# First token list from six half batches instead of eight, the other confident columns in two parts

## The chip, the cores and the metric

The kernel runs on one core of one Trainium2 chip. The metric is the device time of one execution in microseconds (us). Before the change the median of three runs was 1246.0 us, the lowest 1242.64 and the highest 1251.04. One further execution was taken by the hardware profiler, and every duration below is from that one.

## The reference, cut to what matters

A causal seven-tap convolution over the sequence (eight heads of 24 channels, softmax weights) makes 28672 tokens of 192 channels. A router with eight experts gives each token to one expert, greedily by logit, with at most 3584 tokens per expert. Each token goes through the two-layer network of its expert.

```python
out = np.einsum('hk,bskhg->bshg', w, x_unf)            # causal convolution, 7 taps, 8 heads
...
cap = N // E                                           # 28672 // 8 = 3584
logits = x @ w_gate
order = np.argsort(-logits.flatten())
for idx in order:
    tok, e = (int(idx) // E, int(idx) % E)
    if assigned[tok] >= 0 or counts[e] >= cap:
        continue
    assigned[tok] = e
    counts[e] += 1
...
for e in range(E):
    mask = assigned == e
    h = np.maximum(x[mask] @ w1[e], 0.0)               # 192 -> 1024
    out[mask] = h @ w2[e]                              # 1024 -> 192
```

## The kernel before, in words

**Convolution.** The sequence is cut into 16 half batches of 1792 tokens. For each, eight matmuls (one per head, `cv<-X,TH` in the trace, two records each) make the convolution, ScalarE evicts it to `a`, and a DMA stores it to the DRAM tensor `attn`. VectorE transposes `a` to `aT`, TensorE makes logits from that (`pl<-aT`), transposes them (`pt`), and ScalarE writes them into the table `LT` [128 partitions, 8 experts, 256 columns]; each half batch fills 16 columns. `M1` holds the largest logit of each token.

**Routing.** A token whose largest logit is above a sampled threshold `Ts` is confident: it goes to its best expert whatever comes later. The lists of such tokens are made from the columns of `LT`, in parts. For a part, `settle` marks the confident tokens in `F`, `count` counts them per expert, `place` numbers them, `slots` splits the number into a place within 128 and a block, `sort` or `sort4` brings the tokens into that order with one-hot matmuls (VectorE builds the one-hots `oa`, TensorE multiplies), `gather` puts the pieces of all parts together in the table `asm`, and `tokens` turns them into row numbers: `ia` (row of the output) and `ja` (row of `attn`). `sort` is followed by `turn`, which transposes its result on TensorE. `sort4` instead writes its result to the DRAM table `otab` and reads it back transposed (`X<-otab`); `gather` must wait for that read. Its time is guessed by a constant, `TURN = 10.0`, from the last eviction.

Before the change there are two parts of 128 columns. The first part (eight half batches) gives the first list, of which 512 tokens per expert are used (`ia0`, `ja0`). The second part gives the complete confident list (`ia`, `ja`, 2048 per expert). Then `rest` settles all other tokens by seven rounds of threshold search on VectorE (`rounds`, `final`) and makes their list in two halves (`ib`, `jb`, 1536 per expert), each by `sort4`.

**The expert network.** The tokens go through the network in 56 tiles of 512 tokens: tiles 0 to 7 take the first list (one for each expert), tiles 8 to 31 the confident list (three for each), tiles 32 to 55 the rest. Tile i is done in eight steps (f): five matmuls of layer 1 of tile i (`ph`), then eight matmuls of layer 2 of tile i-1 (`y`). ScalarE makes `hh` from `ph`, VectorE `hl`; three buffers hold `ph`. GpSimd gathers the rows of a tile from `attn` two tiles ahead (`xg`), and scatters the results to the output. Weights of a new expert are loaded as `raw` pieces, split into two terms by ScalarE and VectorE or GpSimd, used, and kept in DRAM (`kw`, `kv`) for the later passes.

**What sets the order.** Every engine runs its instructions in the order in which the program writes them. The routing is a chain of generators (`Steps`): at fixed places, between the matmuls of the convolution and of the tiles, `hook` lets the first generator run on for a few steps, as long as a rough running estimate of the engines' times (`Pace`) says that VectorE is not more than a slack ahead of TensorE. So the estimate decides at build time where routing instructions stand among the others. Three places force the chain: before tile 6 gathers for tile 8, `bg.drain(1)` runs whatever is left of the confident list and one step of what follows; before tile 30 gathers for tile 32, `bg.drain()` runs all that is left of `rest`, and takes no account of `TURN`; before tile 1 the last logits are finished. In the convolution, the backlog of transposes and logits is held from half batch 13 on until the first list is made (`LAG`, `got`); then the rows of tiles 0 and 1 are gathered (`first`), and ten heads later, at heads 2 and 5 of a half batch, the operands of tile 0 are transposed on TensorE (`bg<-ident,xg`) and evicted (`todo`).

All instructions that go through the pace estimate carry line L56 in the profile, so they are told apart by the names of their tiles: `bg` is the PSUM tile of every routing matmul.

## Time and profile before

| what | before |
|---|---|
| median of three runs | 1246.0 us |
| profiled execution, its own time | 1251.99 us |
| span from first to last instruction in it | 1250.2 us |
| TensorE busy | 1208.1 us, 97% of the span |
| VectorE busy | 979.4 us, 78% |
| ScalarE busy | 547.4 us, 44% |
| GpSimd busy | 531.7 us, 43% |
| mean granted TensorE clock | 0.994 |

TensorE is nearly always busy, so a microsecond in which it waits, or has one more microsecond of work, is a microsecond at the end. A matmul's end is modelled in the records; how much time a run of matmuls takes is read from the start of the next one. In a timeline row the columns are the start, the busy time, the engine, the tiles (out<-in), the shape, the count, and in brackets the idle time before it and what ended it.

### The profile page before, as it was taken

What the parts mean: (1) busy time and instruction counts of PE and PEld (TensorE: products, weight loads), DVE (VectorE), ACT (ScalarE), POOL (GpSimd) and SP (SyncE); (2) the same over time, 40 slices, a digit from 0 to 9 for tenths busy, and PEclk for the clock granted to TensorE, in tenths of its full rate; (3) what the DMA queues carried; (4) which work ended last, traced back from release to release, by engine and by line L of the source; (5) the groups of instructions that cost most, each with busy time, mean ns of one, the idle gap of its engine ahead of it and who ended that gap; (6) DMA issues with size and microseconds to landing.
All of it is one profiled execution on the core that took longest, in us unless ns stands there. A gap on an engine that the chain in (4) does not pass through costs nothing.

```text
span 1250.2 us, 21752 instructions
## 1 busy us (share of the span) xinstructions
PE 1208.1 (97%) x7702; PEld 1036.5 (83%) x7702; DVE 979.4 (78%) x2131; ACT 547.4 (44%) x1220; POOL 531.7 (43%) x528
## 2 busy tenths in 40 slices
PE   4999989999999999999999989999999999999997
PEld 2445568889988989889888879999999999999996
DVE  7388669889898898989888865777777777777772
ACT  4454555656444544444543333333443333443331
POOL 3000344535455545555454434445444544444522
PEclk9999999999999999999999999999999999999999
DMA  9999889999725463444344563114133222413100
GB/s 221 339 348 310 294 299 316 280 321 302 270 82 155 128 188 113 158 149 149 123 144 135 178 164 121 36 48 154 67 126 107 95 97 96 157 56 137 49 23 28
DMA packets 125188, 205.09 MB, mean 164 GB/s; under 512 B 21440, under 2 KB 85392, under 8 KB 121360
## 3 DMA queue, kind: packets, MB, share of 16 engines
q1 hardware_dynamic: 82464, 127.22, 31.9%
q0 software_dynamic: 21504, 44.07, 11.7%
q10 hardware_dynamic: 21104, 32.34, 7.8%
q8 instruction: 62, 1.02, 0.3%
q14 instruction: 54, 0.44, 0.1%
HBM read 118.64 MB, written 84.93 MB: 163 GB/s over the span
## 4 chain that ended last, share of the span: by engine, by line
PE 85%; DVE 6%; DMA 5%; issue 1%; SPq 1%; ACT 1%; POOL 1%; ACTq 0%; POOLq 0%; DVEq 0%
PE ph L56 40%; PE y L56 38%; PE bg L56 3%; PE cv L56 3%; DMA X<-in_x_dram 2%; DVE X L56 1%; DVE aT L56 1%; DMA wgr<-in_moe_w_gate_dram 1%; DMA raw<-in_moe_w_dram 1%; DMA X<-otab 1%; PE pl L56 1%; DMA xg<-attn,ja 1%; DVE hl L56 0%; PE px L56 0%; DMA otab<-X 0%
## 5 line engine op out<-in xcount | busy, mean ns | idle before, releaser
L56 PE MATMUL y<-w,hh 128*128 128x384 f32 x1792 | 536.8, 355 | 0.0
L56 ACT ACTIVATE hh<-ph 128x512 fp32r<-128x512 f32 x448 | 267.2, 597 | 486.3 <-PE ph L56 485.2
L56 PE MATMUL y<-w,hl 128*128 128x192 f32 x1792 | 449.7, 251 | 0.0
L56 DVE SCALAR_TENSOR_TENSOR hl<-ph,hh 128x512 fp32r<-128x512 f32 x448 | 308.5, 689 | 138.6 <-ACT hh L56 134.0
L56 PE MATMUL ph<-xa,w 128*128 128x512 f32 x1344 | 395.6, 402 | 0.0
L56 PEld LDWEIGHTS y<-w,hl 128*128 128x128 f32 x1792 | 341.7, 191 | 16.4
L56 PEld LDWEIGHTS y<-w,hh 128*128 128x128 f32 x1792 | 337.1, 188 | 20.4 <-issue 2.2
L56 PEld LDWEIGHTS ph<-xa,w 128*128 128x128 f32 x1344 | 218.9, 189 | 20.2 <-issue 1.0
L1348 POOL DMA_INDIRECT out_dram<-yo,ia x128 | 138.9, 1085 | 225.9 <-DVE yo L56 188.1
L1348 POOL DMA_INDIRECT out_dram<-yo,ib x96 | 95.9, 999 | 220.1 <-DVE yo L56 212.7
L56 PE MATMUL ph<-xd,w 128*128 128x512 f32 x448 | 178.9, 399 | 1.3 <-DVE xd L56 1.3
L56 PE MATMUL ph<-xd,dl 128*128 128x512 f32 x448 | 174.6, 390 | 0.2 <-DVE dl L56 0.2
L56 DVE STREAM_TRANSPOSE xs<-xg 32x128 f32<-32x128 f32 (+2 forms) x408 | 164.8, 404 | 6.6
L1273 POOL DMA_INDIRECT xg<-attn,ja x128 | 139.3, 1088 | 47.6 <-issue 40.4
L56 PE MATMUL cv<-X,TH 118*128 118x384 f32 x256 | 101.5, 523 | 19.5 <-DVE TH L56 12.5
L1273 POOL DMA_INDIRECT xg<-attn,jb x96 | 103.4, 1078 | 29.3 <-issue 29.3
L56 ACT ACTIVATE yt<-y 128x192 f32<-128x192 f32 x224 | 73.1, 326 | 94.3 <-PE y L56 92.3
L56 DVE TENSOR_TENSOR yo<-y,yt 128x192 f32<-128x192 f32 x224 | 79.5, 355 | 41.3 <-ACT yt L56 39.2
L56 PEld LDWEIGHTS ph<-xd,w 128*128 128x128 f32 x448 | 84.3, 188 | 21.4 <-DVE xd L56 1.7
L56 PEld LDWEIGHTS ph<-xd,dl 128*128 128x128 f32 x448 | 84.5, 189 | 19.7 <-issue 0.5
L56 PEld LDWEIGHTS cv<-X,TH 118*128 118x128 f32 x256 | 45.3, 198 | 49.9 <-issue 14.1
L56 ACT ACTIVATE a<-cv 128x384 f32<-128x384 f32 x128 | 59.5, 492 | 50.8 <-PE cv L56 33.0
(238 smaller groups left out, 893.1 us busy)
## 6 DMA issues: line engine op xcount, KB each, us to landing
attn<-a ACTq DMA_DIRECT2D x16, 1344.0 KB
w<-kw SPq DMA_DIRECT2D x14, 1536.0 KB
w<-kv SPq DMA_DIRECT2D x14, 1536.0 KB
kw<-w SPq DMA_DIRECT2D x48, 256.0 KB
kv<-w SPq DMA_DIRECT2D x32, 384.0 KB
X<-in_x_dram SPq DMA_DIRECT2D x17, 672.0 KB
X<-in_x_dram ACTq DMA_DIRECT2D x15, 672.0 KB
scr<-xs SPq DMA_DIRECT2D x96, 96.0 KB
```

The lines of the kernel that those rows point to most:

```text
L56: return f(*a, **k)
L1273: self.nc.gpsimd.indirect_dma_start(out=t[:, b], out_offset=None, in_=self.attn[0:rows], in_offset=bass.IndirectOffsetOnAxis(ap=idx[b], ax ...
L1348: st = self.nc.gpsimd.indirect_dma_start(out=self.out, out_offset=bass.IndirectOffsetOnAxis(ap=idx, axis=0), in_=o, in_offset=None, bounds ...
```

## The change

The columns are cut at 96 and 224 (`PARTS`): the first part has the columns of six half batches, the second those of eight, the third those of the last two. `early` makes the first list from part one. `second` makes part two by `sort4`; while its read-back from DRAM is under way, `third` marks and counts part three (before the change, `open`, which takes the confident tokens out of `LT` and `F`, stood there); after the gather of part two, part three is placed, sorted by `sort` in 32 columns, turned and gathered, then `tokens` makes the list, and `open` comes last. `rest` keeps its two halves (`HALVES`). The other edits pass a column offset and a width instead of a half's number.

```diff
+PARTS = ((0, 96), (96, 128), (224, 32))
+HALVES = ((0, 128), (128, 128))
...
-        while z < 128:
+        n = part[1]
+        while z < n:
...
-                if z == 64:
-                    yield from self.columns(h, nt, base)
+                if z == n // 64 * 32:
+                    yield from self.columns(part, nt, bases)
...
             for u in range(4):
                 e = 4 * q + u
-                if base is not None:
-                    PE.matmul(o, b(self.tot[base]), self.ones, start=False, stop=False, skip_group_check=True)
-                PE.matmul(o, b(self.tot[h]), self.U, start=False, stop=(u == 3), skip_group_check=True)
+                for p in bases:
+                    m = p[1]
+                    PE.matmul(o, self.tot[p][:, e:e + 1].to_broadcast([m, 128]), self.ones[0:m, 0:n],
+                              start=False, stop=False, skip_group_check=True)
+                PE.matmul(o, self.tot[part][:, e:e + 1].to_broadcast([n, 128]), self.U[0:n, 0:n],
+                          start=False, stop=(u == 3), skip_group_check=True)
...
-    def lists(self, F, nt, h, base, idx, row, *part, between=None, swap=False):
-        yield from self.place(F, h, base)
-        yield from self.slots(F, h, between is None)
+    def listed(self, F, nt, part, bases, between=None):
+        yield from self.place(F, part, bases)
+        yield from self.slots(F, part, between is None)
         if between is None:
-            yield from self.sort(h, nt, base)
-            yield from self.turn()
+            yield from self.sort(part, nt, bases)
+            yield from self.turn(part[1])
         else:
-            yield from self.sort4(h, nt, base)
+            yield from self.sort4(part, nt, bases)
             yield from between
-        yield from self.gather(nt, base is None)
-        yield from self.tokens(nt, idx, row, *part, swap=swap)
+        yield from self.gather(part[1], nt, not bases)
...
-        def half(h):
-            if h == 0:
-                yield from r.thresh(0.905)
-            yield from r.settle(h)
-            yield from r.count(r.F, h)
-            if h:
-                yield from r.counts(NE)
-            yield from r.lists(r.F, TA, h, 0 if h else None, *((ia, ja) if h else (ia0, ja0, 8, 4)),
-                               between=r.open() if h else None, swap=h == 1)
+        def early():
+            yield from r.thresh(0.905)
+            yield from r.settle(PARTS[0])
+            yield from r.count(r.F, PARTS[0])
+            yield from r.listed(r.F, TA, PARTS[0], ())
+            yield from r.tokens(TA, ia0, ja0, 8, 4)
+
+        def second():
+            yield from r.settle(PARTS[1])
+            yield from r.count(r.F, PARTS[1])
+            yield from r.listed(r.F, TA, PARTS[1], PARTS[0:1], between=third())
+            yield from r.listed(r.F, TA, PARTS[2], PARTS[0:2])
+            yield from r.tokens(TA, ia, ja, swap=True)
+            yield from r.open()
+
+        def third():
+            yield from r.settle(PARTS[2])
+            yield from r.count(r.F, PARTS[2])
+            yield from r.counts(NE)
...
-        bg = Steps(nc, r, (half(0), tail(), half(1), rest()))
+        bg = Steps(nc, r, (early(), tail(), second(), rest()))
```

Since the pace estimate places the steps, the change moves instructions far from its own lines. Three places are shown, each before and after.

The first is TensorE at the end of the convolution. `cv` are the convolution's matmuls, `pl` and `pt` the logits' matmuls and transpose, `bg<-ident,xg` the transposes of tile 0's gathered rows, `ph` the first layer of tile 0. Before:

```order
L56 MATMUL pl<-aT,c_mu 32x128 x8
L56 MATMUL bg<-ident,xg 128x128 x4
L56 MATMUL cv<-X,TH 128x384
L56 MATMUL pl<-aT,c_mu 32x128 x8
L56 MATMUL cv<-X,TH 128x384
L56 MATMUL pt<-ident,L 128x128
L56 MATMUL bg<-ident,xg 64x128 x4
L56 MATMUL ph<-xa,w_1548 128x512 x3
L56 MATMUL ph<-xd,w_1548 128x512
```

and now:

```order
L56 MATMUL pl<-aT,c_mu 32x128 x8
L56 MATMUL bg<-ident,xg 128x128 x4
L56 MATMUL cv<-X,TH 128x384
L56 MATMUL pt<-ident,L 128x128
L56 MATMUL cv<-X,TH 128x384 x2
L56 MATMUL bg<-ident,xg 64x128 x4
L56 MATMUL cv<-X,TH 128x384 x2
L56 MATMUL ph<-xa,w_1576 128x512 x3
L56 MATMUL ph<-xd,w_1576 128x512
```

The two groups of transposes stood two heads before the end and behind the last head; now they stand five and two heads before the end. The gather of the first list (`bg<-c_oh` on TensorE) stood ahead of head 1 of half batch 14 and now stands ahead of head 3 of half batch 13, six heads earlier.

The second is VectorE at the start of tile 6, where the confident list is forced. `LT<-LT,c_mu` and `F<-F,k_b` are `open`, `Ts`, `T`, `c_T` and `X<-LT,c_T` the first step of the rounds, `hl` belongs to the tiles. Before, `open` stood at the end of tile 3 and start of tile 4, among the tiles' work:

```order
L56 TENSOR_SCALAR c_mu<-M_76,Ts 128x256
L56 TENSOR_TENSOR LT<-LT,c_mu 128x1024 x2
L56 SCALAR_TENSOR_TENSOR hl<-ph,hh 128x512
L56 TENSOR_TENSOR w_2889<-raw,w_2889 128x512
L56 SCALAR_TENSOR_TENSOR hl<-ph,hh 128x512
L56 TENSOR_SCALAR k_b<-sl 128x256
L56 TENSOR_TENSOR F<-F,k_b 128x2048
```

Now its second half stands in one block at the start of tile 6:

```order
L56 TENSOR_TENSOR dl<-raw,w_3592 64x512
L56 TENSOR_TENSOR LT<-LT,c_mu 128x1024
L56 TENSOR_SCALAR k_b<-sl 128x256
L56 TENSOR_TENSOR F<-F,k_b 128x2048
L56 TENSOR_SCALAR Ts_3691<-Ts 128x1
L56 MEMSET T 128x8
L56 TENSOR_SCALAR c_T<-T 128x8
L56 SCALAR_TENSOR_TENSOR X_3698<-LT,c_T 128x256 x2
L56 SCALAR_TENSOR_TENSOR hl<-ph,hh 128x512
```

Six instructions of the routing stand between two of the tiles' there, where before at most three stood together.

The third is TensorE around the last gather of `rest`. `bg<-oa,X` are the sort's last matmuls, `bg<-iq,ones` opens the gather's PSUM tile, `bg<-c_oh,X` reads the table that comes back from DRAM. Before, the gather stood in tile 29, inside layer 1 of its step 4, 23 `ph` and 40 `y` matmuls behind the last sort block:

```order
L56 MATMUL y<-w_7888,hh 128x384
L56 MATMUL y<-w_7888,hl 128x192
L56 MATMUL ph<-xa,w_8385 128x512 x3
L56 LDWEIGHTS ones
L56 MATMUL bg<-iq,ones 128x192
L56 LDWEIGHTS X_9383
L56 MATMUL bg<-c_oh,X_9383 128x24
```

Now the last sort block stands one tile later, in step 7 of tile 29, and the forced drain before tile 30 puts the gather right behind it:

```order
L56 MATMUL bg<-oa,X_9233 32x128
L56 MATMUL y<-w_7978,hh 128x384
L56 MATMUL y<-w_7978,hl 128x192
L56 MATMUL y<-w_7978,hh 128x384
L56 MATMUL y<-w_7978,hl 128x192
L56 MATMUL y<-w_7978,hh 128x384
L56 MATMUL y<-w_7978,hl 128x192
L56 MATMUL y<-w_7978,hh 128x384
L56 MATMUL y<-w_7978,hl 128x192
L56 LDWEIGHTS ones
L56 MATMUL bg<-iq,ones 128x192
L56 LDWEIGHTS X_9699
```

Between the last sort block and the gather stand 0 `ph` and 8 `y` matmuls now.

## The prediction

> **What bounds the kernel now.** I read the slices of the span first, then stretches, then the timelines of single engines at the places the change touches.

> ```profile
> PE   4999989999999999999999989999999999999997
> ```

> TensorE is full from about 150 us to the end; what it gains or loses counts in full. Its idle time sits in few places. One is the passage from the convolution to the first tile:

> ```profile
> 150.00:160.00 10.00, 8.35 (x98) 4.05 (x96) 5.28 (x8) 3.42 (x9) 8.44 (x9) 1.00 0.73 249
> ```

> The columns are TensorE, its weight loads, VectorE, ScalarE, GpSimd, granted clock, share and rate of the DMA engines: 1.65 us of ten idle. TensorE's timeline names the waits:

> ```profile
> 155.93 1.00 PE L56 MATMUL bg<-ident,xg 128*128 128x128 f32 x3
> 158.46 0.33 PE L56 MATMUL bg<-ident,xg 128*128 128x128 f32 x1 [1.53 <-DMA xg<-attn,ja]
> ...
> 161.16 0.94 PE L56 MATMUL ph<-xa,w 128*128 128x512 f32 x3
> 163.41 0.51 PE L56 MATMUL ph<-xd,w 128*128 128x512 f32 x1 [1.31 <-DVE xd L56]
> ```

> The rows of tile 0 come late (1.53 us), and so does their last operand (1.31 us). The first list is late for both; the rest of the convolution is bound by TensorE's own work.

> The second place is the gather of the confident list, whose table makes a trip through DRAM:

> ```profile
> 239.36 1.22 PE L56 MATMUL bg<-oa,X 128*32 128x128 bf16 x32
> ...
> 251.79 0.28 PE L56 MATMUL bg<-iq,ones 128*128 128x256 bf16 x1
> 253.71 0.55 PE L56 MATMUL bg<-c_oh,X 128*128 128x32 bf16 x16 [1.64 <-DMA raw<-in_moe_w_dram]
> ```

> The row names a weight transfer, but the matmul reads `X`, which the same queue brings: the table came some 13 us after the sort's last block, and 1.64 us late.

> The third is the same trip at the end of `rest`, in tile 29:

> ```profile
> 730.21 1.19 PE L56 MATMUL bg<-oa,X 128*32 128x128 bf16 x32
> 731.33 0.44 PE L56 MATMUL y<-w,hh 128*128 128x384 f32 x1
> ...
> 732.55 0.88 PE L56 MATMUL ph<-xa,w 128*128 128x512 f32 x3
> ...
> 742.42 0.26 PE L56 MATMUL bg<-iq,ones 128*128 128x192 bf16 x1
> 746.00 0.58 PE L56 MATMUL bg<-c_oh,X 128*128 128x24 bf16 x16 [3.32 <-DMA X<-otab]
> ```

> From the end of the last sort block (731.33, where the next matmul starts) to the table (746.00) are 14.67 us; TensorE had 11.1 us of tile work for them. SyncE's queue shows why it is that long:

> ```profile
> 730.67 1.81 SPq L1396 DMA_DIRECT2D scr<-xs  x4
> ...
> 736.00 0.59 SPq L546 DMA_DIRECT2D otab<-X  x1
> 736.70 5.47 SPq L563 DMA_DIRECT2D X<-otab  x8
> ```

> The write of the table (736.00) stands behind the scratch transfers of a transposed tile, and the eight reads behind the write. The wait has a second price, the clock:

> ```profile
> 745.00:750.00 5.00, 4.00 (x28) 3.74 (x29) 3.29 (x11) 0.60 (x1) 0.00 (x0) 0.50 0.87 341
> 750.00:755.00 5.00, 5.00 (x27) 4.47 (x25) 2.97 (x12) 1.53 (x3) 0.99 (x1) 0.85 0.00 0
> ```

> The granted clock is 0.50, and 0.85 over the next five microseconds, so half until about 751.5: 5.5 us of work at half speed from 746.0, or 2.75 us lost. That stop cost 3.3 + 2.75 = 6.1 us.

> **The change part by part.**

> *The convolution.* 32 columns of the first list's sort leave it. Their price stands in the old program's last rows of that list:

> ```profile
> 132.11 2.07 PE L56 MATMUL bg<-X,oa 128*128 128x16 bf16 x32
> 134.03 2.18 PE L56 MATMUL cv<-X,TH 118*128 118x384 f32 x6
> 136.05 1.16 PE L56 MATMUL bg<-identb,X 128*128 128x128 bf16 x16
> 137.04 2.15 PE L56 MATMUL cv<-X,TH 118*128 118x384 f32 x6
> 139.04 0.27 PE L56 MATMUL bg<-iq,ones 128*128 128x256 bf16 x1
> 139.15 0.55 PE L56 MATMUL bg<-c_oh,X 128*128 128x32 bf16 x16
> 139.55 1.86 PE L56 MATMUL cv<-X,TH 118*128 118x384 f32 x5
> ```

> From start to next start: 32 sort matmuls 1.92 us (0.06 each), the turn 0.99, the gather 0.51. TensorE saves 1.9 us, with narrower `place` matmuls 2.0. The first list's gather stands six heads earlier, ahead of head 3 of half batch 13. Heads 3 to 5 began at 134.03, so in the old timeline that place is 134.0; the turn now stands before it (+1.0), and the 2 us are saved: about 133, against 139.04, a lead of 6 us. The rows of tile 0 landed at 158.4 and would land at 152.4. The transposes that read them stand three heads earlier: at 155.93 less 3 x 0.36 (six records in 2.15 us, two a head), less the 2.0 saved and a logits group or two, so 151 to 153. The 1.53 us wait shrinks to 1.4 at worst and goes at best. The list's last step decides:

> ```profile
> 141.71 1.26 DVE L56 TENSOR_SCALAR m_i<-m_f,off 128x32 int32<-128x32 f32 x1
> ```

> ```profile
> 141.65 1.29 POOL L1254 TENSOR_TENSOR w<-raw,w 128x512 fp32r<-128x512 f32 x1 [32.54 <-ACT w L56]
> ```

> ```profile
> L56 DVE TENSOR_SCALAR m_i<-m_f,off 128x128 int32<-128x128 f32 x1 | 0.3, 281 | 0.0
> ```

> This step of `tokens` took 1.26 us in 32 columns while GpSimd split a weight, and 0.28 us in 128 columns elsewhere. In the new order the list comes before GpSimd's first split, so some 2 us more of lead are likely, and I count the wait as gone. [...]

> The second group of transposes stands two heads before the end, so the operand that cost 1.31 us is made under those heads. Start of tile 0: 2.0 + 1.5 + 1.3 = 4.8 us earlier. Bounds: 2.0 (both waits stay, on something else) and 7 (the other idle time around 150 goes too). GpSimd now gathers eight times before it splits tile 0's first weights; I cost that at nothing, since tile 0 starts some 18 us behind the list.

> *The tiles' stretch.* What left the convolution comes back there, with a third part's fixed work: 32 sort matmuls 1.92, a turn 0.99, a gather 0.51, 26 matmuls of `place` and 15 small ones of `count`, `columns` and `counts` at 0.06 each, 2.5. Sum 5.9 us, in a stretch in which TensorE has no idle time but the 1.64: all of it counts. Bounds 4 and 7.

> *The gather of part two.* Between sort and table stand 22 `ph` before and after, and 8 `y` fewer, which is 1.22 us (731.33 to 732.55 above), but `third` adds 16 small matmuls, 1.0 us. The wait stays 1.6 us: 0, between -1.6 and +2.

> *Forced end at tile 6.* Six routing instructions stand ahead of tile 6's first `hl`:

> ```profile
> L56 DVE TENSOR_TENSOR LT<-LT,c_mu 128x1024 f32<-128x1024 f32 x2 | 2.4, 1222 | 0.0
> ...
> L56 DVE TENSOR_TENSOR F<-F,k_b 128x2048 bf16<-128x2048 bf16 x1 | 1.2, 1226 | 0.0
> ```

> 1.22 + 1.23 and five smaller steps, about 4 us. Three `ph` buffers cover some three steps of 2.3 us; TensorE then waits 0 to 3 us. I take 1.

> *Forced end at tile 30.* Here the cover goes. The last sort block stands one tile later, and its gather now waits behind 8 `y` matmuls: 1.22 us. SyncE's rows around it are as before (scratch transfers, write, eight reads, then a weight load), so the table again needs 14.67 us: TensorE waits 14.67 - 1.22 - 0.26 = 13.2 us instead of 3.3, so +9.9. The half clock was paid before and is paid once again: 0, within 1 us. [...] Half came after 3.3 us idle here; restoring took 5.5. [...] Behind the gather, VectorE makes `jb`, and GpSimd's gather for tile 32 waits with the scatters of tile 29 behind it. Tile 32's rows have a whole tile, 18 us, to arrive: no cost. Bounds of the stop: +5 (write and reads from 736.00 to 746.00 alone are 10 us, so 8.5 idle) and +12.

> Sum: -4.8 + 5.9 + 0 + 1 + 9.9 = +12.0 us on the profiled execution's 1251.99, so 1264. That execution is 6.0 us above the median of the runs shown; the same shift on 1246.0 gives 1258. Five terms with these bounds, not all at one end: +6 to +18, 1252 to 1264.

> **The rivals.**

> *VectorE becomes the bound in tiles 4 to 6.* It gets the third part's work:

> ```profile
> 129.88 2.49 DVE L56 TENSOR_TENSOR oa<-irep,q 128x1024 bf16<-128x1024 bf16 x4
> ```

> ```profile
> 280.00:300.00 20.00, 20.00 (x120) 18.19 (x119) 18.72 (x35) 11.70 (x24) 9.81 (x8) 1.00 0.98 344
> ```

> Four one-hot builds (2.5) and some 22 steps near 0.28 make 8.7 us, where it is busy 18.7 of 20 us. Against: the steps are spaced, and TensorE shows no idle time there. If it decides, 7 us more: 1265.

> *The early start is swallowed by weights.*

> ```profile
> 182.82 0.63 ACT L56 ACTIVATE w<-raw 128x512 fp32r<-128x512 f32 x1 [4.66 <-DMA raw<-in_moe_w_dram]
> ```

> ScalarE waited 4.66 us for a weight piece of tile 1's expert. If that transfer does not move with the tiles, the 4.8 us are lost: 1263. Against: its issue follows the splits of tile 0, which move.

> *The table at tile 30 comes sooner.* With the 8.5 us wait worked out above, the sum is +7: 1253.

> *Not slower: the table is nearly there when the gather comes.* The place is the same; each microsecond sooner is one off the sum. The sum is zero where the wait is 13.2 - 12.0 = 1.2 us, that is, a table 2.7 us behind its last sort block: 1246. Against: the trip took 14.67 and some 13 us in the two rows above.

> *The change does not do what it says:* the first list is too short and the general path runs. In the reference's data, the first six half batches hold at least 845 tokens per expert above a threshold that gives the largest expert 0.905 of its 3584, and 512 are needed: no chance given.

> **How the numbers follow.** A measurement of this kernel tells about 1% from no change, here 1233.5 to 1258.5. Forecast 0.57 (the sum lies at the bound: 0.30 within, 0.27 slower), VectorE 0.15, weights 0.11, table sooner 0.10, not slower 0.07. Slower: 0.27 + 0.14 + 0.09 = 0.50; faster 0.04 out of the last case; within 1%: 0.46. Likeliest time 1258. The range takes the forecast's bounds, the 1253 of the early table, and the 1265 of the late VectorE with 2 us for its own bounds: 1249 to 1267.

> **What would show it.** Right: first `ph` near 156.5, with no idle time ahead of its `xd`; the third part's `bg` matmuls in tiles 3 and 4 at 0.06 each; one wait near 13 us at about 750, on `X<-otab`, then half clock for some 5 us. Wrong: a `ph` that waits for `hl` for several microseconds in tiles 4 to 6; a wait at tile 30 under 10 us; a first `ph` after 159.

## The result, and the profile after

The changed kernel takes 1267.55 us (median of 4 runs, 1265.51 to 1270.01), the kernel before beside it 1247.76 (4 runs): a ratio of 1.0159, 95% interval 1.0128 to 1.0191. Its profiled execution takes 1270.01 us with a span of 1268.1, which is 18.0 us more than before. The prediction had +12.0. The direction was right; the size was not, and neither was the account of the start and of the gather of part two.

The slices of the span show where it went: the slice of TensorE with the last gather has a 6 (761 to 793 us) where before had an 8 (719 to 750 us), and the clock row has two dips, to 8 (from 159 us) and to 7 (from 761 us), where before had none.

```profile
PE   4999989999999999999999996999999999999997
...
PEclk9999989999999999999999997999999999999999
```

Where in the span the 18 us arise is read from the first eviction of layer 2 (`yt<-y` on ScalarE) in the same tile of both programs. For tiles 0, 2 and 6 the rows of before, then of after:

```profile
185.90 0.32 ACT L56 ACTIVATE yt<-y 128x192 f32<-128x192 f32 x1
...
227.73 0.33 ACT L56 ACTIVATE yt<-y 128x192 f32<-128x192 f32 x1
...
309.27 0.33 ACT L56 ACTIVATE yt<-y 128x192 f32<-128x192 f32 x1
```

```profile
186.27 0.32 ACT L56 ACTIVATE yt<-y 128x192 f32<-128x192 f32 x1
...
227.71 0.33 ACT L56 ACTIVATE yt<-y 128x192 f32<-128x192 f32 x1 [1.10 <-PE y L56]
...
319.48 0.33 ACT L56 ACTIVATE yt<-y 128x192 f32<-128x192 f32 x1 [0.51 <-PE y L56]
```

So +0.4 us at tile 0, 0.0 at tile 2 and +10.2 at tile 6; by tile 30 it is +18.2 (798.50 against 780.34), and there it stays. Three stops of TensorE and one stretch of added work make it up. TensorE's timeline of after, at the start, at the gather of part two, and at the last gather:

```profile
154.81 0.33 PE L56 MATMUL pt<-ident,L 128*128 128x128 f32 x1 [1.36 <-ACT L L56]
...
157.71 1.16 PE L56 MATMUL ph<-xa,w 128*128 128x512 f32 x3
...
174.52 1.65 PE L56 MATMUL ph<-xa,w 128*128 128x512 f32 x3 [3.19 <-DVE hl L56]
...
248.27 0.55 PE L56 MATMUL bg<-c_oh,X 128*128 128x32 bf16 x16 [1.21 <-DMA kw<-w]
248.67 0.22 PE L56 MATMUL bg<-F,U 128*128 128x128 bf16 x1
...
251.16 0.69 PE L56 MATMUL y<-w,hh 128*128 128x384 f32 x1
...
758.89 0.44 PE L56 MATMUL y<-w,hh 128*128 128x384 f32 x1
...
772.28 0.58 PE L56 MATMUL bg<-c_oh,X 128*128 128x24 bf16 x16 [11.91 <-DMA X<-otab]
```

The first `ph` is 3.45 us earlier than before (161.16), and a stop of 3.19 us that did not exist before takes this back. The wait of 1.21 us at 248.27 is put down to a store of weights, but the matmul reads `X`, which the same queue brings (SyncE issues the eight `X<-otab` from 237.89, stores of `kw` from 245.35). The stretches behind the three stops, with the columns as before (the granted clock is third from the right):

```profile
174.00:182.00 8.00, 7.46 (x21) 5.47 (x22) 5.97 (x10) 3.82 (x7) 0.72 (x1) 0.57 0.97 378
249.00:257.00 8.00, 8.00 (x45) 6.91 (x45) 5.37 (x16) 1.12 (x2) 1.58 (x2) 0.57 1.01 353
764.00:779.00 15.00, 6.72 (x35) 5.89 (x36) 4.14 (x18) 0.60 (x1) 1.81 (x2) 0.54 0.72 199
```

A mean of 0.57 over 8 us is half clock for 8 x 2 x 0.43 = 6.9 us, and 0.54 over 15 us for 13.8. Taken as half speed, the first two cost an estimated 3.4 us each, nearly all of it work. The third began in the wait; from 772.28 to 778.4 it ran over work, which cost 3.1 us by the same estimate, about as much as the 2.7 of before.

The start's stop comes from weights. GpSimd, SyncE and ScalarE of after:

```profile
138.58 1.25 POOL L1286 DMA_INDIRECT xg<-attn,ja  x1 [29.41 <-DVE aT L56]
...
149.69 1.29 POOL L1267 TENSOR_TENSOR w<-raw,w 128x512 fp32r<-128x512 f32 x1
```

```profile
163.92 2.86 SPq L1227 DMA_DIRECT2D raw<-in_moe_w_dram  x1
```

```profile
172.73 0.52 ACT L56 ACTIVATE w<-raw 128x384 fp32r<-128x384 f32 x1 [4.63 <-DMA raw<-in_moe_w_dram]
```

Eight gathers stand ahead of the first split, which came at 141.65 before and comes at 149.69 now. SyncE stores each split weight before it asks for the next raw piece, so the last piece of tile 0's second weights is asked for 3.2 us later than before (160.73) and holds ScalarE for 4.63 us with `hh` behind it. SyncE's own issues are slow there as well: the five that start from 154.79 to 163.92 take 1.7 to 2.9 us each; the last five of before (158.76 to 160.73) took 0.3 to 0.6. The row 248.67 to 251.16 is the third part's `place`: 26 small matmuls in 2.5 us, without tile work in between.

### The profile page after: what moved, and what is told of

Read it like the earlier page. It is cut to its first block, busy times and chain, and to the rows that moved or that the text cites. A ratio compares the mean times of both kernels' runs of the same rounds, so it can differ in the third digit from the quotient of the medians.

```text
span 1268.1 us, 21924 instructions
## 1 busy us (share of the span) xinstructions
PE 1219.3 (96%) x7774; PEld 1045.9 (82%) x7774; DVE 977.6 (77%) x2153; ACT 549.0 (43%) x1223; POOL 529.2 (42%) x530
## 4 chain that ended last, share of the span: by engine, by line
PE 82%; DMA 7%; DVE 6%; SPq 1%; issue 1%; ACT 1%; POOL 1%; ACTq 0%; DVEq 0%; POOLq 0%
PE ph L56 38%; PE y L56 37%; PE bg L56 3%; PE cv L56 3%; DMA X<-in_x_dram 2%; DVE X L56 1%; DVE aT L56 1%; DMA raw<-in_moe_w_dram 1%; DMA wgr<-in_moe_w_gate_dram 1%; DMA otab<-X 1%; DMA scr<-xs 1%; PE pl L56 1%; DMA kw<-w 1%; DVE hl L56 1%; DMA xs<-scr 1%
## 5 line engine op out<-in xcount | busy, mean ns | idle before, releaser
L56 PE MATMUL y<-w,hh 128*128 128x384 f32 x1792 | 538.9, 356 | 0.0
L56 ACT ACTIVATE hh<-ph 128x512 fp32r<-128x512 f32 x448 | 267.3, 597 | 497.8 <-PE ph L56 495.3
L56 PE MATMUL y<-w,hl 128*128 128x192 f32 x1792 | 450.2, 251 | 0.0
L56 DVE SCALAR_TENSOR_TENSOR hl<-ph,hh 128x512 fp32r<-128x512 f32 x448 | 308.1, 688 | 136.0 <-ACT hh L56 131.6
L56 PE MATMUL ph<-xa,w 128*128 128x512 f32 x1344 | 398.9, 405 | 3.2 <-DVE hl L56 3.2
L56 PEld LDWEIGHTS y<-w,hl 128*128 128x128 f32 x1792 | 342.5, 191 | 16.4
L56 PEld LDWEIGHTS y<-w,hh 128*128 128x128 f32 x1792 | 338.0, 189 | 19.3 <-issue 1.0
L56 PEld LDWEIGHTS ph<-xa,w 128*128 128x128 f32 x1344 | 220.2, 190 | 25.5 <-DVE hl L56 4.4
L56 PE MATMUL ph<-xd,w 128*128 128x512 f32 x448 | 178.9, 399 | 0.0
L56 PE MATMUL ph<-xd,dl 128*128 128x512 f32 x448 | 175.2, 391 | 0.0
L56 DVE STREAM_TRANSPOSE xs<-xg 32x128 f32<-32x128 f32 (+2 forms) x408 | 164.8, 404 | 6.7 <-DVE hl L56 0.2
L56 PE MATMUL cv<-X,TH 118*128 118x384 f32 x256 | 101.0, 521 | 19.5 <-DVE TH L56 12.1
L56 DVE TENSOR_TENSOR yo<-y,yt 128x192 f32<-128x192 f32 x224 | 79.3, 354 | 44.5 <-ACT yt L56 42.6
L56 ACT ACTIVATE yt<-y 128x192 f32<-128x192 f32 x224 | 73.0, 326 | 93.4 <-PE y L56 89.9
L56 PEld LDWEIGHTS ph<-xd,w 128*128 128x128 f32 x448 | 84.7, 189 | 20.1 <-issue 1.0
L56 PEld LDWEIGHTS ph<-xd,dl 128*128 128x128 f32 x448 | 84.7, 189 | 20.0 <-issue 0.5
L56 PEld LDWEIGHTS cv<-X,TH 118*128 118x128 f32 x256 | 45.2, 197 | 49.5 <-issue 13.4
L56 ACT ACTIVATE a<-cv 128x384 f32<-128x384 f32 x128 | 58.9, 493 | 52.9 <-PE cv L56 25.6
```

The costliest lines, as they stand in the source:

```text
L56: return f(*a, **k)
```

## The experiments

Times are medians, with the ratio to the kernel before on the same chip. The kernel before took 1248.4 to 1248.6 us beside the first eleven runs and 1255.5 beside the last three, so those are read by their ratios. In an expectation, the theory is the account that a run puts to the test, and the rival another account that would give another time or another trace.

**e1: rows of tile 1 behind the splits.**

```diff
-            for e in range(2):
-                ff.gather(e, [ja0[:, e, b:b + 1] for b in range(4)], NTOK // 2, P)
+            rows(0)
...
+                if (i, h) == (15, 0):
+                    rows(1)
```

> Only the order on GpSimd is changed: the rows of tile 0 are gathered first, then come the splits of tile 0's four weight pieces, then the rows of tile 1 (at half batch 15, head 0). Theory (the stop of 3.19 us at 174.5 in tile 0 and the half clock behind it come from the eight gathers that stand ahead of the first split at 149.69, so that SyncE asks for the last raw piece of the second weights only at 163.92): the first split starts near 144 to 146, the four splits are over by about 151, the last raw piece is asked for before 158, TensorE has no stop between 160 and 185 and the granted clock stays 1.00 there; the lead of 4.7 us reaches tile 2, and the time is 1267.6 - 4.7 = 1263 (1261 to 1265). Rival (the transfers are bound by the DMA engines, whose share is 0.98 to 1.00 from 160 to 190): the piece lands near 172.7 whatever its place in the queue, the stop stays above 2 us, and the time is 1267 (1266 to 1269).

1260.56 us, 1.0094 [1.0065, 1.0122]. GpSimd splits at 142.64, and the first eviction comes 6.5 us earlier than in the changed kernel:

```profile
142.64 1.30 POOL L1267 TENSOR_TENSOR w<-raw,w 128x512 fp32r<-128x512 f32 x1
```

```profile
179.77 0.32 ACT L56 ACTIVATE yt<-y 128x192 f32<-128x192 f32 x1
```

The clock is 1.00 from 160 to 190, and the last piece is asked for at 152.06. The theory holds and the rival falls; the time is 0.4 us below the theory's range. The start varies between executions: that eviction comes at 182.94 to 186.27 in the seven profiles with the changed start (mean 184.6), at 182.35 to 186.54 in the six with the old one (184.6), at 178.18 to 179.77 in the three with e1's order (179.2). All seven with the changed start stop for `hl` between 170 and 177 us, for 2.5 to 4.2 us together; none of the nine others does for more than 0.3. So the changed start gains nothing, and in e1's order it gains 5 us.

**e2: rows of tile 32 four steps later** (`f == (4 if i == 30 else 0)` ahead of the gather).

> Only the gather of the rows of tile 32 is moved, from the start of tile 30 to its step 4, so that nothing forces the end of the last list at the start of tile 30. Theory (the wait of 11.91 us is the table's trip of 13.4 us against 1.5 us of work in between): about 10.4 us of tile work now stand between the last sort block and the table's gather, the wait is 13.4 - 10.4 - 0.3 = 2.7 us, and the half clock behind it stays or goes: 1267.6 - 9.2 = 1258.4 with it, 1255.5 without. Rival (the late rows of tile 32 take its place): they are asked for some 9 us later against a tile's 18 us, VectorE waits for them in tile 31 with that tile's hl behind it, TensorE waits up to 4 us there or at tile 32, and the time is 1261 to 1263. Second rival (the table is bound by what else is queued): the wait stays near 12, 1267.

1260.4 us, 1.0089 [1.0061, 1.0117]. The wait is the trip less its cover; the late rows cost nothing:

```profile
771.83 0.58 PE L56 MATMUL bg<-c_oh,X 128*128 128x24 bf16 x16 [3.25 <-DMA X<-otab]
```

**e3 and e4: the third part's `place` apart from the gather; more time for the table.** e3 adds `yield nc.pe + 3.0` ahead of each of the two groups, e4 sets `TURN = 13.5`.

> The two groups of 13 place matmuls of the third part no longer follow the gather of part two at once; each waits for 3 us of the planner's TensorE time, so that tile matmuls stand between gather and groups. The same instructions, 26 small matmuls in a row broken in two. Theory (half clock from 249.3 to 256.9 comes from the stretch of small matmuls without tile work that follows a wait of 1.2 us): the clock stays 1.00 between 245 and 262, 7.5 us of half speed or 3.7 us go, and the time is 1264 (1263 to 1265). Rival (the wait at the gather alone lowers the clock): half clock stays for about as long, and the time is 1267.6 within 1.

> The planner lets the table of a list rest for 13.5 instead of 10 of its microseconds before it is read; the 26 place matmuls still follow the gather of part two at once. Theory (wait and small matmuls together make the half clock): with some 12.6 us of tile work in place of 9.7 the wait of 1.21 us goes, the clock stays 1.00 at the gather, -1.2 - 3.7, and the last stop in tile 30 gets up to 1.2 us longer since its last sort block moves next to it: 1263 to 1264. Rival (the row of small matmuls alone lowers the clock): half clock for some 7 us stays behind the gather although nothing waits, and the time is 1267 (1266 to 1268).

e3: 1271.18 us, 1.0177 [1.0149, 1.0206]. Here the wait at the gather is 1.39 us and the clock stays 1.00 from 240 to 260, as the theory said; but the third list, now later, meets the forced end at tile 6, and TensorE waits for `hl`, with half clock for 3.4 us:

```profile
300.33 1.21 PE L56 MATMUL ph<-xa,w 128*128 128x512 f32 x3 [2.87 <-DVE hl L56]
```

That is the prediction's forced end at tile 6 at its upper bound (0 to 3 us), which the changed kernel just escapes. The time fits neither theory nor rival. e4: 1265.72 us, 1.0131 [1.01, 1.0162]. The wait goes, but the second group then waits 1.08 us for `asm`, and 3.4 us of half clock stay: neither theory nor rival as written. The last stop did not grow but shrank, from 11.91 to 8.47 us, and the trip took 8.7 us: the write of its table, 0.7 us behind the sort's end (760.02), had nothing ahead of it to wait for:

```profile
760.75 0.34 SPq L557 DMA_DIRECT2D otab<-X  x1
761.18 4.45 SPq L574 DMA_DIRECT2D X<-otab  x8
```

**e5: all covers at once** (e1's order; the groups one hook apart; 13.5 for the second and the last table; rows of tile 8 at step 2 of tile 6, of tile 32 at step 5 of tile 30).

> The changed kernel with every cost that was found taken away at once: rows of tile 1 gathered behind the splits; the place groups of the third part one hook apart from the gather ahead of them; 13.5 instead of 10 planner's microseconds between a table's write and its gather, in the second list and in the last one; the rows of tile 8 gathered at step 2 of tile 6 and those of tile 32 at step 5 of tile 30, so that no list is forced to its end there. Theory (the stops are separate and add up): from 1267.6, the start gives 7.0; the gather of part two 1.2 of wait and 3.4 of half clock; the last stop 11.9 - 0.5 of wait and 3.0 of half clock: 1267.6 - 26.0 = 1241.6 (1240 to 1244). Rival (the third list, now later by a third of a tile, runs into the forced end at tile 6): a wait for hl of about 3 us at the start of tile 6 with 2 us of half clock, 1246 to 1248.

1250.16 us, 1.0023 [1.001, 1.0037]. The time lies above both theory and rival: with every cost covered that had been found, the changed kernel is still 0.2% slower than the kernel before. The last stop is down to 0.34 us and the start keeps its lead, but a stop like the rival's came: `open`'s steps (5.5 us of VectorE at 290.4) stand ahead of `xa`:

```profile
297.27 0.60 PE L56 MATMUL px<-ident,xg 128*64 128x128 f32 x4 [2.79 <-DVE xa L56]
```

**e6: the kernel before with `TURN = 13.5`.**

> The kernel before with nothing changed but the rest of a table, 13.5 instead of 10 planner's microseconds. Theory (its own two waits, 1.64 us at the second list and 3.32 us with half clock in tile 29, are of the same kind as the changed kernel's): both waits and the half clock of 5.4 us go, -1.6 - 3.3 - 2.7 from 1248: 1240.4 (1239 to 1242.5), so that the changed kernel without its stops is no better than the kernel before without its own. Rival (the last list ends later and is forced at tile 30 with its wait as long as before): 1246 to 1248.

1245.87 us, 0.9983 [0.9972, 0.9995]: 2.5 us of the 7.6 expected. The last wait shrinks only to 2.04 us, although 14 us of work now cover it, because the trip grew: sort end 732.77 to table 749.43 is 16.7 us. A weight load stands ahead of the table's write on SyncE, and the reads behind it take 12.15:

```profile
732.45 0.58 SPq L1231 DMA_DIRECT2D w<-kw  x1
733.13 0.45 SPq L1232 DMA_DIRECT2D dl<-kd  x1
733.62 0.58 SPq L546 DMA_DIRECT2D otab<-X  x1
734.25 12.15 SPq L563 DMA_DIRECT2D X<-otab  x8
```

**e7: `open` last, no third part.**

```diff
+PARTS = ((0, 128), (128, 128))
...
-            yield from r.listed(r.F, TA, PARTS[2], PARTS[0:2])
...
-            yield from r.settle(PARTS[2])
-            yield from r.count(r.F, PARTS[2])
```

> One part of the change alone: two parts of 128 columns as in the kernel before, no third part, but the steps of open stand behind tokens as in the change. Theory (it is the third part and not the order that takes the cover from the last gather): the last sort block stands five steps sooner than in the changed kernel, at step 4 of tile 29, with 8.1 us of tile work up to the gather at tile 30; the wait is 13.4 - 8.1 - 0.3 = 5.0 us instead of 3.3, half clock once as before, the gather of the second list loses 0.6 us of its cover: 1248 + 2.3 = 1250.3 (1249 to 1252). Rival (the order alone does the harm): the wait at tile 30 is above 9 us, 1254 or more.

1240.54 us, 0.9936 [0.9913, 0.9959]: this half of the change alone makes the kernel before faster. The last sort block stands at step 4 of tile 29 as expected, but the wait is 0.37 us, not 5.0, and the time fits neither theory nor rival. The trip is short there (sort end 741.44 to 750.15, 8.7 us), and nothing stands ahead of the write; the scratch transfers are over or not yet issued:

```profile
742.19 0.33 SPq L557 DMA_DIRECT2D otab<-X  x1
742.57 5.04 SPq L574 DMA_DIRECT2D X<-otab  x8
748.56 1.79 SPq L1409 DMA_DIRECT2D scr<-xs  x4
```

**e8 and e9: the scratch reads behind the table's**, for tile 31 in the changed kernel, for tile 30 in the kernel before (`if i != 31: self.back(i)`, and `self.back(31)` a step into the next tile; `back` holds the two `xs<-scr`).

> In the changed kernel the two reads of tile 31's scratch, which stand on SyncE between the four scratch writes and the write of the last table, are issued one step into tile 30, behind the table's reads; nothing else moves. Theory (the trip of 13.4 us is some 8 us of the table itself, as 742.19 to 750.15 in the run with open last, and the rest is SyncE standing at the scratch reads until the scratch writes have landed): the table's write is issued near 760.2 instead of 763.1, the wait at tile 30 is 7.6 to 8.8 us instead of 11.9, half clock as before, 1263.3 to 1264.5. Rival (the write follows the scratch writes in the same rings and lands no sooner): the wait stays above 11 us, 1267.

> The same edit in the kernel before, for tile 30's scratch, with the last table's write now right behind the scratch writes. Theory: the write is issued near 732.5 instead of 736.0, the table is there 8 to 9.2 us later, at 740.5 to 741.7, and the gather comes at 742.7: the wait of 3.3 us and its half clock (2.7) go, 1248.4 - 6.0 = 1242.4 (1241 to 1244). Rival (the write lands no sooner): wait of 3 us and half clock stay, 1248.

e8: 1260.27 us, 1.0092 [1.0074, 1.011]. The wait is 8.03 us, inside the theory's 7.6 to 8.8, and the trip 9.5 us. The time is 3 us below the theory's: this execution also had 3.41 us less of half clock at each of the three stops.

```profile
765.22 0.60 PE L56 MATMUL bg<-c_oh,X 128*128 128x24 bf16 x16 [8.03 <-DMA X<-otab]
```

e9: 1250.44 us, 1.0008 [0.9994, 1.0022]. The table's wait went, and another came: the scratch reads now stood behind the weight load (1536 KB), and ScalarE waited for them with `hh` behind it. TensorE stopped for 2.39 and 0.67 us, with 6.8 us of half clock:

```profile
747.48 0.63 ACT L56 ACTIVATE xa<-xs 128x512 fp32r<-128x512 f32 x1 [6.79 <-DMA xs<-scr]
```

**e13: the same, ahead of the weight load** (`if (i, f) == (28, 7): self.back(30)` ahead of `wsplit`).

> The kernel before with the two reads of tile 30's scratch behind the table's eight reads, but now ahead of the weight load that followed them. Theory: the table's write goes out near 732, the table is there by 741.7 and the scratch reads by 742, the gather at 742.7 waits for nothing, and no later stop takes its place: 1248.4 - 6.0 = 1242.4 (1241 to 1244). Rival (the eight reads hold the scratch back long enough for ScalarE to wait for it with hh behind it): a stop of 2 us or more with half clock at 745 to 755, 1247 to 1250.

0.9946 [0.9928, 0.9965], 1249.73 against 1255.54: 5.8 us by the medians, 6.8 by the ratio, with 6.0 expected. No half clock is left between 45 us and the end:

```profile
747.36 0.56 PE L56 MATMUL bg<-c_oh,X 128*128 128x24 bf16 x16 [0.29 <-DMA X<-otab]
```

The way there was another, though. The write went out at 738.82, not near 732, because ScalarE had the block's result ready only at 738.79, 3.5 us behind the block's end (735.32) instead of 0.7; why is not shown. The trip was 12.0 us, 2.6 less than before, and the gather came 0.4 us later behind its block.

**e10 and e11: slack of 2.0 instead of 1.8** (`SS = (2.0, 3)`), alone and with e1's order.

> One number in the changed kernel: routing steps are let in with 2.0 instead of 1.8 planner's microseconds of VectorE's lead from the tiles on, which puts the last sort block at step 2 of tile 29 instead of step 7, ahead of the scratch transfers of that tile, with 11 us of tile work behind it. Theory (the place of that block is what the last stop costs, by the cover and by the queue): no wait and no half clock at the last gather, -11.9 - 3.0 from 1267.6, so 1252.7 (1251 to 1255). Rival (a tighter routing pushes VectorE, which is busy 8 to 10 of 10 us in tiles 1 to 6): the last stop goes, but waits for hl or xa in tiles 3 to 8 take back 3 us and more: 1256 or above.

> The slack of 2.0 and, as in the first experiment, the rows of tile 1 gathered behind the four splits. Theory (the stop at the start and the last stop are separate): the 7.0 us of the first experiment come on top, 1245.7 (1244 to 1248). What then stays of the change is the work of the third part, its half clock in tile 3 and the lead of the start. Rival (the lead at the start ends in a stall of VectorE or of the weights in tiles 1 to 6): 1250 to 1253.

e10: 1256.11 us, 1.0051 [1.0031, 1.0071]; e11: 1252.85 us, 1.0035 [1.0021, 1.0049]. The last stop went in both (0.64 and 0.89 us), but the first table of the last list moved too, onto a tile's scratch transfers: in e10 its sort ends at 712.3, behind the scratch writes of 711.77, and its trip is 13.8 us. The same queue, another table:

```profile
726.12 0.58 PE L56 MATMUL bg<-c_oh,X 128*128 128x24 bf16 x16 [3.50 <-DMA X<-otab]
```

So the numbers lie near the rivals', for a reason that neither named. e1's order gained 3.3 us here, not 7.0. The last table shows that the writes ahead are not all: nothing stands right ahead of it, and still its reads take 8.23 us in e10 (8.33 in e11) and the trip 12.0 (12.2). A weight load was asked for some 5 us earlier; that it is the cause is not shown.

```profile
751.16 0.33 SPq L557 DMA_DIRECT2D otab<-X  x1
751.54 8.23 SPq L574 DMA_DIRECT2D X<-otab  x8
```

**e12: the `place` row behind tile work** (e3's line for the first group alone, with 1.0).

> In the changed kernel the 26 place matmuls of the third part stay in one row, but four pairs of y matmuls stand between them and the gather of part two with its wait. Theory (half clock needs the wait and the row of small matmuls close together): the wait of 1.2 to 1.8 us at the gather stays, the clock is 1.00 from 245 to 262, and the time is some 3.4 us below the changed kernel's: 1264 (1262 to 1265). Rival (a row of 26 small matmuls is enough by itself): half clock for 5 us or more behind the row, 1267 (1266 to 1268).

1.0123 [1.0101, 1.0145]. The theory falls, but not to the rival: half clock began at 247.4, right behind a wait of 1.88 us and ahead of the row, and lasted through it, 11 x 2 x 0.47 = 10.3 us. The time can't tell them apart, since this interval overlaps the changed kernel's own (1.0128 to 1.0191).

```profile
247.17 0.57 PE L56 MATMUL bg<-c_oh,X 128*128 128x32 bf16 x16 [1.88 <-DMA kw<-w]
```

```profile
247.00:258.00 11.00, 10.83 (x69) 9.49 (x70) 4.87 (x15) 1.23 (x3) 1.80 (x2) 0.53 0.79 271
```

**e14: e7 with 12 for the second table.**

> Two parts of 128 columns with the steps of open last, as in the seventh experiment, and 12 planner's microseconds between the second list's table and its gather. Theory: the 0.7 us wait at that gather goes and nothing else moves: 1240 (1238.5 to 1241.5), faster than both kernels. Rival (the later list shifts what follows it): a new wait in tiles 4 to 8 or at tile 30, 1243 or above.

1.0021 [1.0004, 1.0038], 1257.23 us against 1255.54: the rival. The steps of `tokens`, on VectorE from 250.3 to 255.2, now stand ahead of `xa`, and TensorE waits 2.22 us for it at 257.38; the last table's wait is 1.75 instead of 0.37. Each has 3.4 us of half clock. e7's gain rests on where its lists fall; one number moves it away.

## Why the prediction was wrong

Its sum against the profile, the steps as it put them:

| step | predicted | measured |
|---|---|---|
| start of tile 0 | -4.8 | first `ph` -3.45, at tile 2 0.0 |
| third part's work, tiles 2 to 6 | +5.9 | +7.2 |
| gather of part two | 0 | wait -0.4, half clock +3.4 |
| forced end at tile 6 | +1 | 0 |
| forced end at tile 30 | +9.9 | +8.0 |
| sum | +12.0 | +18.2 |

The 7.2 is the 10.2 between tiles 2 and 6, less 3.4 of half clock, plus 0.4 by which the wait at the gather was shorter (1.21 for 1.64). The 8.0 is 18.2 less 10.2. The measured column is one execution's; the first eviction of tile 0 alone spreads over 3.3 us in the seven profiles with the same start.

**The step that failed first** is "GpSimd now gathers eight times before it splits tile 0's first weights; I cost that at nothing, since tile 0 starts some 18 us behind the list". The 18 us were compared with the list, not with the chain that hangs on the splits: store, next raw piece, ScalarE. The lead was made much as predicted and lost at 174.5. The list's step at 136.49 took 0.23 us instead of 1.26, the first gather of rows starts 7.8 us sooner (138.58 for 146.34), and neither the rows nor `xd` are waited for. The 1.35 us that are missing from the 4.8 are a new wait: 1.36 us for the logits' transpose at 154.81. e1 undoes that one step and gets 7.0 us back by the medians; in its profile tile 0's first eviction is 6.5 us sooner than in the changed kernel's, 4.8 sooner than the mean of the seven. In its outcome this is the prediction's rival of weights that swallow the start, given 0.11, though the piece that came late is tile 0's own and not tile 1's; its counter-argument, that the issue follows the splits "which move", had the splits moving the right way, and they moved 8 us back.

**The second** is the gather of part two at 0 us. The wait was right (1.21 us for 1.6). That such a wait, with the third part's row of small matmuls right behind it, can cost three microseconds more by the clock was left out: before, 1.64 us there had cost none. The last section shows the difference.

**The third part's work** was mis-sized: 7.2 for 5.9, just outside its bound of 7. The 26 `place` matmuls took 2.2 us at full clock (e11, 238.90 to 241.12), 0.085 each instead of 0.06: half of the excess.

**Tile 30** was right in mechanism: e2 gives the wait back with cover, and the half clock is paid once again. 1.3 of the 1.9 us by which the size was off are the trip, which was 13.39 us (758.89 to 772.28) instead of 14.67. The prediction saw the write stand behind the scratch transfers, but took the length of the trip as given. It is not: the last table took 8.7 us in e4 and e7, with nothing ahead of the write that it waited for, 9.5 in e8 behind the scratch writes alone, 13.1 to 14.7 in before, after, e1, e2, e3, e5 and e12 behind the scratch writes and reads, and 16.7 in e6 behind a weight load. The 12.0, 12.2 and 10.1 us of e10, e11 and e14, with nothing right ahead of the write, show that this order is not the whole of it. "SyncE's rows around it are as before" was true.

**Tile 6**: no cost, within the bounds. The block ahead of the first `hl` is eight instructions, not six, and takes 3.8 us (297.87 to 301.67), as estimated, but no `ph` waits for it; e3 and e5 show a stop of 2.8 to 2.9 us as soon as the lists come a third of a tile later.

The median lies 0.55 us above the range, whose bounds let each rival come alone. Here the lost start and the half clock at the gather came together; that the miss is not larger is due to the two forced ends, which cost 2.9 us less than forecast. The kernel before also took 1.8 us more beside the changed one than the 1246.0 that the forecast starts from.

## What to carry to other kernels

When an instruction is moved ahead of others on an engine, follow the chain of each one that it delays, to its last waiter, before calling the delay free. The length of the trip through DRAM depended here on the place in the queue where it started: look at what stands ahead of the write and of the reads, since here the same trip took 8.7 us in one order and 14.7 in another. And time the halves of a change apart: one half of this one is a gain of 0.6%, as long as its lists fall where e7 puts them.

## What the runs showed of the hardware

Read along the grid, the traces show what e3, e4 and e12 left open. Behind 160 us, TensorE was busy for at most 0.46 of the stretch in 22 stretches at full clock, and half clock followed all of them; it followed three of the eight between 0.47 and 0.58. Above that it followed only six, and each of them holds the third part's row of small matmuls or a piece of it. This is a count over the sixteen profiles; no experiment was made for it, and what makes the clock fall is not shown. At the gather of part two, the stretches of the grid in the kernel before, then in the changed one:

```profile
249.72:253.13 3.41, 2.35 (x14) 1.89 (x12) 2.21 (x4) 1.80 (x4) 1.20 (x1) 1.00 1.11 178
253.13:256.55 3.42, 2.84 (x30) 2.66 (x31) 2.22 (x9) 1.06 (x2) 0.00 (x0) 1.00 1.06 394
```

```profile
245.96:249.37 3.41, 2.20 (x31) 1.55 (x29) 2.49 (x10) 1.29 (x3) 2.80 (x3) 1.00 0.93 241
249.37:252.79 3.42, 3.42 (x25) 3.00 (x24) 1.68 (x7) 0.52 (x1) 1.21 (x2) 0.50 1.05 365
```

The 1.64 us of before fall on two stretches, 1.06 and 0.58 us, and nothing follows. In the changed kernel the 1.21 us and the first 0.70 us of the row fall into one. Half clock also followed the row with next to no wait: in e10 it lies whole in one stretch with 0.06 us idle, and half clock follows (so too in e1 and e8, with 0.17 and 0.07 us); in e11 it lies across two stretches, and none follows. So the rival of e4 and e12, that the row is enough by itself, was right in the three executions in which one stretch holds it whole:

```profile
244.65:248.06 3.41, 3.35 (x47) 2.90 (x48) 1.59 (x5) 0.00 (x0) 2.61 (x3) 1.00 0.87 281
248.06:251.47 3.41, 3.41 (x12) 2.95 (x12) 3.03 (x12) 1.86 (x4) 1.03 (x1) 0.50 1.02 333
```

```profile
237.10:240.51 3.41, 3.41 (x45) 2.83 (x43) 2.31 (x9) 0.60 (x1) 2.59 (x3) 1.00 0.92 289
240.51:243.92 3.41, 3.41 (x25) 3.07 (x24) 2.33 (x9) 1.64 (x4) 2.41 (x3) 1.00 0.99 308
243.92:247.34 3.42, 3.42 (x22) 3.08 (x22) 3.38 (x8) 1.18 (x4) 0.08 (x1) 1.00 1.03 352
```

At the last gather, with 0.3 to 0.9 us of wait (e5, e7, e10, e11, e13) the clock stayed full, with 1.75 us and more (e14, e6, before, after) it halved. At half clock four pairs of `y` matmuls took 2.08 us from start to next start (after, 774.99 to 777.07), at full clock 1.12 (785.75 to 786.87), so 3.41 us of half clock over work cost an estimated 1.6 us, a little less than the 1.7 of half speed.
